# A fused attention and MLP-mixer kernel on one core: two stores move to Gelu's buffers, a PSUM copy is cut in halves, reciprocals are spread a turn later, and row maxima are placed a little later behind VectorE

## The chip, the core and the metric

The kernel runs on one core of a Trainium2 chip. The core has TensorE (PE in the profile, with its weight loads as PEld), VectorE (DVE), ScalarE (ACT), GpSimd (POOL), and SyncE (SP), which here only issues transfers. Each engine works through its own queue in order, and semaphores tie the queues together. Matmuls write to PSUM, which has eight banks of 128 partitions x 512 float32 values.

The metric is the device time of one execution in microseconds. Before the change the median of three runs is 1082.11 us (1080.81, 1086.48 and 1082.11).

## The reference

The input x has 2048 tokens of width 448. A gate per token mixes an attention block of 16 heads (28 wide) with an MLP that has a layer norm in front and 1792 hidden units. All is float32.

```python
def _A_ref(x, wqkv, wo):
    qkv = (x @ wqkv).reshape(B, S, 3, H, Dh).transpose(2, 0, 3, 1, 4)
    q, k, v = qkv[0], qkv[1], qkv[2]
    scores = jnp.einsum("bhqd,bhkd->bhqk", q, k) * (Dh ** -0.5)
    p = _softmax(scores, axis=-1)
    o = jnp.einsum("bhqk,bhkd->bhqd", p, v)
    return o.transpose(0, 2, 1, 3).reshape(B, S, D) @ wo

def _B_ref(x, w1, b1, w2, b2):
    y = _layernorm(x, axis=-1)
    h = _gelu(jnp.einsum("bsd,df->bsf", y, w1) + b1)
    return jnp.einsum("bsf,fd->bsd", h, w2) + b2

g = _sigmoid((x * gate_w).sum(-1, keepdims=True))
return g * _A_ref(x, A_wqkv, A_wo) + (1 - g) * _B_ref(x, B_w1, B_b1, B_w2, B_b2)
```

## The kernel before

To stay near float32 the kernel splits an operand into a high part (fp32r, a reduced form) and a low part, the rest, and adds three products: high by high, high by low, low by high.

The work has two stretches. The **first** makes queries, keys and values and then the whole MLP. TensorE's 128 rows are used as four strips of 32 rows; each strip works on its own share of an output tile, and four matmuls, one a strip, run side by side. The MLP goes block by block, four blocks of 512 tokens: 14 "up" tiles (hidden units, class `Up`), each emptied by ScalarE with Gelu into a tile `h` and copied to its high part, and then four "down" tiles (class `Down`, 128 tokens each), emptied by ScalarE into a tile `gb` (L398) and stored to memory (`gbs`, L401) until the end. `h` has two buffers, and `gb` has two. Only in the last block do the third and fourth down tile (`self.i > 1`) use the buffers of `h`. When a tile is asked for, the next buffer in turn is given, and its first writer waits until the last reader, a store here, is done with it.

The order of TensorE's matmuls in this stretch is made while the program is built, by a planner (`Strips`). It keeps a clock for each strip and a time at which each engine is free, with a fixed cost for each kind of work, and gives a strip the first work that is ready by these clocks. Work left over for it are the **row maxima** (`RowMax`): the softmax needs for each query the largest score over 2048 keys, so a matmul of queries against 512 keys is made into PSUM bank 6 or 7 (L212) and VectorE reduces it to one column (L214). There are 1024 of these in all. `rowmax` (L497 to L508) places one when a strip comes by and one of the two banks is free by the planner's reckoning, which is when VectorE is done (`self.dve`, 0.65 for a reduction) and a margin later. What is not placed here is made in the second stretch.

The **second** stretch is attention. A unit is one head's scores of 128 keys against 512 queries: three matmuls and an exp on ScalarE. There are 1024 units, 64 for each of 16 combinations of four heads and 512 queries (`n`). Work goes by **turns** (`turn_of`): a turn has five, six or seven units in two halves, and among their passes stand row maxima that are still owed (`lone`): three in a turn of five (at places 0, 3 and 5; the first and third use bank 6), two in a turn of six (places 0 and 5, both bank 6). As long as more than a certain number are owed, the size is five. After the scores of a turn come that turn's entries of an agenda (transfers and small work that was put down for it), and then **batches**: the products of four units' probabilities with values, 128 keys for four heads (`batch`), summed in bank 7 over 16 batches. When the last of the 16 is done, `valued` runs: `finish_a` copies bank 7 to `ob` on VectorE (L1026), and SyncE gathers the row sums out of it (`lt`). Two turns after that `finish_b` takes reciprocals on VectorE, stores them to memory (`rls`) and loads them four times, spread over 32 partitions each (`rc`, L1037). Four turns after, `finish_c` multiplies `ob` by `rc` on GpSimd. In the last group of heads the result is split and projected with the output weights on TensorE (`project`, L1004 to L1006).

Of the kernel before, what the change touches and what calls it, by code (L numbers as in the profile page):

```python
# [15 lines left out]
P = 128  # L16
# [3 lines left out]
DH = 28  # L20
F = 1792
NG = 4
CH = 512
NC = S // CH
# [11 lines left out]
def kernel(ctx: ExitStack, tc: tile.TileContext, xt, wqk, wv, wo, xk, w1, b1, w2, b2,  # L36
                          ident_d, sel_d, out):
    nc = tc.nc
# [21 lines left out]
    rls = dram.tile([NG * NC, 4, CH], F32, name="rls")  # L60
# [101 lines left out]
    class RowMax:  # L162
# [64 lines left out]
        def close(self, n):  # L227
            mf, mt = self.mf[n % 2], self.mt[n % 2]
            nc.vector.reduce_max(mf[:, 0:16], self.mx[n % 2].rearrange("p j i k -> p (j i) k"), axis=AX)
            nc.vector.transpose(mt, mf)  # L230
# [138 lines left out]
    class Down(Piece):  # L369
# [21 lines left out]
            return st.hready.get((self.c, f, p), 1e9) > now or self.c == 0 and st.w2ready.get(f, 1e9) > now  # L391

        def close(self, st, now):
            if self.c == NC - 1 and self.i > 1:
                gb = mhp[0].tile([P, CH], F32, name="h", bufs=2)[:, :D]
            else:
                gb = mhp[0].tile([P, D], F32, name="gb", bufs=2)
            nc.scalar.activation(gb, bk[:, self.bank, :D], AF.Copy)  # L398
            st.use("act", now + 0.2, 0.56)
            st.free[self.bank] = st.act + 0.1  # L400
            nc.scalar.dma_start(gbs[self.c * TPC + self.i], gb)  # L401
            st.use("act", now, 0.5)

    class Strips:
# [28 lines left out]
        def at(self, t, fn, **uses):  # L433
            self.tasks.append((t, self.count, fn, uses))
            self.count += 1
# [61 lines left out]
        def rowmax(self, s, now):  # L497
            if now < self.hot[s] or not rowmax.ready(s):
                return False
            if rowmax.cnt[s] > 5 + min(rowmax.cnt):  # L500
                return False
            b = min(self.rm, key=lambda b: self.rm[b])
            if self.rm[b] > now:
                return False
            ends = rowmax.one(s, bk[:, b])
            self.t[s] = now + 0.232
            self.use("dve", now + 0.45, RM)
            self.rm[b] = self.dve + 0.1  # L508
            for kind, n, j in ends:
                if kind == "q":  # L510
                    self.at(now + 6.0, lambda n=n, j=j: rowmax.load_q(n, j))
                elif kind == "k":
                    def load(n=n, j=j):
                        rowmax.load_k(n, j)
                        self.hot[j] = self.get(self.clock + 0.6, 224) + 1.0

                    self.at(now + 1.5, load)
                    self.hot[j] = 1e9
                else:
                    self.at(now + 0.5, lambda n=n: rowmax.close(n), dve=0.45)  # L520
                    self.at(now + 3.0, lambda n=n: rowmax.store(n))
            return True
# [370 lines left out]
    for i, key in enumerate(load):  # L893
        r = slots[i % 8]
# [48 lines left out]
    def turn_bank(i):  # L943
        return (i + shift) % 6
# [47 lines left out]
    def split_o(g, c, o):  # L992
        if c not in ohs:
            ohs[c] = ao.tile([P, NG, CH], F32R, name="oh"), ao.tile([P, NG, CH], F32R, name="ol")
        h, l = (t[:, g] for t in ohs[c])
        nc.gpsimd.tensor_copy(h, o)
        nc.gpsimd.tensor_sub(l, o, h.bitcast(F32))
# [20 lines left out]

    pv = bk[:, 7]
    obs = {}  # L1020

    def finish_a(n):
        ob = ao.tile([P, CH], F32, name="ob", bufs=1)
        lt = ao.tile([P, CH // 32], F32, name="lt")
        obs[n] = ob, lt
        nc.vector.tensor_copy(ob, pv)  # L1026
        nc.sync.dma_start(lt, ob[DH:P:32, :])

    def finish_b(n):
        ob, lt = obs[n]  # L1030
        rc = ao.tile([P, CH], F32, name="rc", bufs=1)
        obs[n] = ob, rc
        nc.vector.reciprocal(lt, lt)
        r = rls[n]
        nc.sync.dma_start(r.rearrange("j (a b) -> (j a) b", b=CH // 32), lt)
        for j in range(4):
            nc.sync.dma_start(rc[32 * j:32 * j + 32], r[j].partition_broadcast(32))  # L1037

    def finish_c(n):
        g, c = divmod(n, NC)  # L1040
        ob, rc = obs.pop(n)
        if g < NG - 1:
            nc.gpsimd.tensor_mul(ot[g][:, c * CH:(c + 1) * CH], ob, rc)
            return
        nc.gpsimd.tensor_mul(ob, ob, rc)
        split_o(g, c, ob)
# [53 lines left out]
    def valued(n, turn):  # L1100

        g, c = divmod(n, NC)
        if n == NG * NC - 1:
            finish_last(n)
            return
        finish_a(n)
        at(turn + 2, lambda: finish_b(n))
        at(turn + 4, lambda: finish_c(n))
        if g == NG - 1:
            for i in range(TPC):  # L1110
                tail.append((turn + 6 + i, c * TPC + i))
# [7 lines left out]
    def lone(s, b, turn):  # L1119
        if not rowmax.ready(s) or turn < cold[s]:  # L1120
            return
        for kind, n, j in rowmax.one(s, bk[:, b]):
            if kind == "q":
                at(turn + 1, lambda n=n, j=j: rowmax.load_q(n, j))
            elif kind == "k":
                at(turn + 1, lambda n=n, j=j: rowmax.load_k(n, j))
                cold[j] = turn + 5
            else:
                at(turn + 1, lambda n=n: rowmax.close(n))
                at(turn + 2, lambda n=n: rowmax.store(n))  # L1130

    def turn_of(u, turn):

        left = UNITS - u
        owed = rowmax.left()
        size = 5 if owed and owed > 2 * ((left - 104) // 6) + 6 * sixes[0] else 6
        sixes[0] = size == 6
        if not owed and not (tail and tail[0][0] <= turn + 1):
            size = 7
        size = min(left, size)  # L1140
        na = min(4 if size == 7 else 3, size)
        nb = size - na
        for x in range(u, u + size):
            n = x // 64
            if n not in begins:
                begins.add(n)
                begun(n, turn)
        extra = {5: ((0, 3, 6), (3, 1, 5), (5, 2, 6)), 6: ((0, 3, 6), (5, 2, 6))}.get(size, ())
        if size == 7:
            sevens.append(turn)  # L1150
        place = (lambda i: i) if sevens else turn_bank
        if turn in projected:
            extra = extra[1:]
        for half, first, count in ((0, 0, na), (1, na, nb)):
            for p in range(3):
                for x, o, b in extra:
                    if x == 3 * half + p:
                        lone((u + o) % 4, b if b == 6 else turn_bank(b), turn)
                for i in range(first, first + count):
                    n, k = divmod(u + i, 64)  # L1160
                    k, j = divmod(k, 4)
                    r = slice(32 * j, 32 * j + DH + (p == 0))
                    ks = slice(k * P, (k + 1) * P)
                    w = (khi, klo, khi)[p][n // NC]
                    q = (qh, qh, ql)[p][n % 3]
                    nc.tensor.matmul(bk[:, place(i)], w[r, ks], q[r], start=(p == 0), stop=(p == 2), skip_group_check=True)  # L1166
            if count:
                t = ap.tile([P, 4 - half, CH], F32, name=f"p{half}")
                b = place(first)
                nc.scalar.activation(t[:, :count], bk[:, b:b + count], AF.Exp, scale=SCALE)  # L1170
                for i in range(count):
                    prob[u + first + i] = t[:, i]
        return size

    def batch(b, turn, sl=slice(0, CH)):
        n, k = divmod(b, NT)
        for j in range(4):
            nc.tensor.matmul(bk[32 * j:32 * j + 32, 7, sl], vg[n // NC][:, k, 32 * j:32 * j + 32], prob[4 * b + j][:, sl],  # L1178
                             start=(k == 0), stop=(k == NT - 1), skip_group_check=True)
        if k == NT - 1 and sl.stop == CH:  # L1180
            valued(n, turn)
            return True
        return False
# [3 lines left out]
    while b < UNITS // 4:  # L1187
# [12 lines left out]
        while 4 * b + 4 <= before and quota:  # L1200
# [7 lines left out]
            b, begun_half = b + 1, False  # L1208
# [59 lines left out]
```

## Time and profile before

| what | value |
|---|---|
| median of 3 runs | 1082.11 us |
| profiled execution | 1083.55 us |
| its span (first to last instruction) | 1081.8 us |
| TensorE busy | 1068.8 us, 13450 matmuls |
| VectorE busy | 740.8 us, of that 673.7 in 1024 reductions (L214) |
| ScalarE busy | 634.0 us, of that 481.1 in exp (L1170) |
| GpSimd busy | 368.3 us |
| first score of attention | 452.2 us after the start |
| granted clock of TensorE | 1.00, 0.98 after 1010 us |

A row of the timeline or of the groups names the line of the kernel, the engine, the operation, and the tile written and read (`bk` is PSUM, all eight banks under one name); a timeline row begins with its start and its duration in us, and ends with the idle time before it and what ended it. A merged row ends in xN. In a row of waits stand the waiting and the releasing work, then us in total, times, and the longest. In a row of windows each engine's busy time in the stretch is followed by its count. The ends of matmuls are modelled, and matmuls of different strips overlap.

### The profile page before, as it was taken

The page shows a single profiled execution, that of the slowest core. Times are in us where ns is not written, and L with a number is a line of the kernel's source. Part 1 is how long each engine was busy: PE and PEld are TensorE (multiplying, and loading weights), DVE is VectorE, ACT ScalarE, POOL GpSimd, SP SyncE. Part 2 cuts the span into 40 slices and gives each one's busy share as a digit, 9 for nine tenths or more (in the row PEclk, how much of TensorE's full clock was granted, in tenths as well). Part 3 has the DMA queues.
Part 4 walks back from the last instruction along what each step waited for, and adds up shares of the span by engine and source line. Part 5 has one row for each costly group of instructions (what it writes and reads, how often), then busy time and mean ns, then how long its engine had stood idle before and what let it go on. Part 6 is the DMA issues. An engine that isn't in the chain of part 4 may idle for free.

```text
span 1081.8 us, 31072 instructions
## 1 busy us (share of the span) xinstructions
PE 1068.8 (99%) x13450; PEld 725.4 (67%) x13450; DVE 740.8 (68%) x1186; ACT 634.0 (59%) x654; POOL 368.3 (34%) x388
## 2 busy tenths in 40 slices
PE   9999999999999999999999999999999999999997
PEld 6999999999999899844444444444444444464555
DVE  4899998999999999876667655676664444422102
ACT  5234463042142033288788788778888888857671
POOL 4565577336244037441001101300110332444431
PEclk9999999999999999999999999999999999999999
DMA  6696433212100104220000011310000301011111
GB/s 232 214 269 217 168 111 104 77 46 61 45 7 7 46 12 118 92 77 18 25 11 27 16 31 38 78 41 6 25 26 23 71 27 50 25 55 36 61 47 67
DMA packets 47785, 73.20 MB, mean 68 GB/s; under 512 B 13840, under 2 KB 28816, under 8 KB 46848
## 3 DMA queue, kind: packets, MB, share of 16 engines
q1 hardware_dynamic: 33888, 39.11, 12.4%
q0 software_dynamic: 5120, 16.89, 5.5%
q10 hardware_dynamic: 8640, 15.21, 3.9%
q8 instruction: 105, 1.72, 0.7%
q14 instruction: 32, 0.26, 0.1%
HBM read 51.75 MB, written 19.31 MB: 66 GB/s over the span
## 4 chain that ended last, share of the span: by engine, by line
PE 95%; ACT 2%; DMA 2%; DVE 1%; issue 1%; SPq 0%; DVEq 0%; ACTq 0%
PE bk L488 34%; PE bk L1178 22%; PE bk L1166 18%; PE bk L212 15%; PE bk L1004 1%; ACT p L1170 1%; PE bk L1005 1%; PE bk L1006 1%; DMA gbs<-gb 1%; PE bk L920 1%; DMA first<-in_xt 1%; ACT gb L398 0%; DVE ob L1026 0%; PE bk L948 0%; DVE mx L214 0%
## 5 line engine op out<-in xcount | busy, mean ns | idle before, releaser
L214 DVE TENSOR_REDUCE mx<-bk 128x1 f32<-128x512 f32 x1024 | 673.7, 688 | 221.8 <-PE bk L212 178.6
L1170 ACT ACTIVATE p<-bk 128x1536 f32<-128x1536 f32 (+1 forms) x381 | 481.1, 1315 | 125.8 <-PE bk L1166 125.1
L212 PE MATMUL bk<-kd,qd 28*128 28x512 f32 x1024 | 449.8, 441 | 0.6 <-DVE mx L214 0.2
L212 PEld LDWEIGHTS bk<-kd,qd 28*128 28x128 f32 x1024 | 186.0, 182 | 179.7 <-DVE mx L214 115.1
L488 PE MATMUL bk<-yh,w1f 32*128 32x512 f32 x1568 | 192.9, 393 | 2.2 <-ACT gb L398 2.2
L488 PE MATMUL bk<-yl,w1f 32*128 32x512 f32 x784 | 167.4, 392 | 0.0
L488 PEld LDWEIGHTS bk<-yh,w1f 32*128 32x128 f32 x1568 | 154.6, 183 | 4.9 <-ACT gb L398 3.4
L488 PE MATMUL bk<-w2h,hh 32*128 32x448 f32 x896 | 145.0, 366 | 0.0
L488 PE MATMUL bk<-w2l,hh 32*128 32x448 f32 x896 | 144.1, 363 | 0.0
L1178 PE MATMUL bk<-p,va 128*32 128x512 f32 (+1 forms) x1144 | 130.2, 556 | 0.0
L1178 PE MATMUL bk<-p,vb 128*32 128x512 f32 (+1 forms) x1184 | 129.2, 542 | 0.0
L363 POOL TENSOR_TENSOR hl<-h,hh 128x512 fp32r<-128x512 f32 x56 | 72.4, 1305 | 137.2 <-ACT hh L356 99.7
L840 POOL CAST yh<-yl 128x512 fp32r<-128x512 f32 x16 | 9.8, 611 | 288.0 <-DMA yl<-qk 131.2
L488 PEld LDWEIGHTS bk<-yl,w1f 32*128 32x128 f32 x784 | 105.8, 183 | 0.3
L488 PEld LDWEIGHTS bk<-w2l,hh 32*128 32x128 f32 x896 | 103.1, 183 | 0.3
L488 PEld LDWEIGHTS bk<-w2h,hh 32*128 32x128 f32 x896 | 102.7, 183 | 0.4
L1166 PE MATMUL bk<-yh,ka 29*128 29x512 f32 x512 | 101.1, 483 | 0.5 <-ACT p L1170 0.5
L1166 PE MATMUL bk<-yh,kb 29*128 29x512 f32 x512 | 96.5, 480 | 1.7 <-ACT p L1170 1.7
L488 PE MATMUL bk<-w2h,hl 32*128 32x448 f32 x896 | 93.1, 362 | 0.0
L398 ACT ACTIVATE gb<-bk 128x448 f32<-128x448 f32 x14 | 7.6, 545 | 136.8 <-PE bk L488 129.7
L1166 PE MATMUL bk<-yh,la 28*128 28x512 f32 x512 | 83.4, 393 | 0.0
L488 PEld LDWEIGHTS bk<-w2h,hl 32*128 32x128 f32 x896 | 82.4, 183 | 0.3
(141 smaller groups left out, 1604.5 us busy)
## 6 DMA issues: line engine op xcount, KB each, us to landing
qk<-qo ACTq DMA_DIRECT2D x28, 256.0 KB
raw<-in_xt SPq DMA_DIRECT2D x17, 256.0 KB
vs<-vt ACTq DMA_DIRECT2D x16, 256.0 KB
rc<-rls SPq DMA_DIRECT2D x60, 64.0 KB
bxr<-in_xk POOLq DMA_DIRECT2D x8, 448.0 KB, 6.4
acc<-gbs SPq DMA_DIRECT2D x16, 224.0 KB
out_y<-acc SPq DMA_DIRECT2D x16, 224.0 KB
qd<-qk SPq DMA_DIRECT2D x60, 56.0 KB
```

The lines of the kernel that those rows point to most:

```text
L212: nc.tensor.matmul(ps, self.qd[n % 2][r, i * P:(i + 1) * P], self.kd[r, k * 512:(k + 1) * 512], start=True, stop=True)
L214: nc.vector.reduce_max(self.mx[n % 2][:, j, i, k:k + 1], ps, axis=AX)
L363: nc.gpsimd.tensor_sub(hl[f], h, hh[f].bitcast(F32))
L488: mm = nc.tensor.matmul(bk[:, x.bank, :n], a, b, start=x.first, stop=(len(x.rem) == 1 and m == len(ops) - 1), skip_group_check=True)
L840: nc.gpsimd.tensor_copy(h, l.bitcast(F32))
L920: nc.tensor.matmul(bk[:, b], w, v, start=(i == 0), stop=(i == len(ops) - 1), skip_group_check=True)
L1004: nc.tensor.matmul(po, h, woh[:, g], start=(g == 0), stop=False, skip_group_check=True)
L1005: nc.tensor.matmul(po, h, wol[:, g], start=False, stop=False, skip_group_check=True)
L1006: nc.tensor.matmul(po, l, woh[:, g], start=False, stop=(g == NG - 1), skip_group_check=True)
L1166: nc.tensor.matmul(bk[:, place(i)], w[r, ks], q[r], start=(p == 0), stop=(p == 2), skip_group_check=True)
L1170: nc.scalar.activation(t[:, :count], bk[:, b:b + count], AF.Exp, scale=SCALE)
L1178: nc.tensor.matmul(bk[32 * j:32 * j + 32, 7, sl], vg[n // NC][:, k, 32 * j:32 * j + 32], prob[4 * b + j][:, sl], start=(k == 0), stop=(k = ...
```

## The change

There are four parts.

1. The third and fourth down tile of every block, not only of the last one, are emptied into the buffers of `h`.
2. The planner's margin after which a row maximum's bank counts as free is 0.15 instead of 0.1. This is a number in the planner's reckoning and no instruction; it moves the places of row maxima in the first stretch, and what is placed around them.
3. The copy of bank 7 is made in two halves of 256 columns. The second half, and the gather of the row sums behind it, comes in the next turn, after that turn's first row maximum (or at the turn's end, if none stands there).
4. The four loads that spread the reciprocals come a turn later than the store of the reciprocals, through a function of their own.

```diff
@@ class Down, close @@
-            if self.c == NC - 1 and self.i > 1:
+            if self.i > 1:
                 gb = mhp[0].tile([P, CH], F32, name="h", bufs=2)[:, :D]
             else:
                 gb = mhp[0].tile([P, D], F32, name="gb", bufs=2)
@@ Strips.rowmax @@
-            self.rm[b] = self.dve + 0.1
+            self.rm[b] = self.dve + 0.15
@@
+    late = []

     def finish_a(n):
         ob = ao.tile([P, CH], F32, name="ob", bufs=1)
         lt = ao.tile([P, CH // 32], F32, name="lt")
         obs[n] = ob, lt
-        nc.vector.tensor_copy(ob, pv)
-        nc.sync.dma_start(lt, ob[DH:P:32, :])
+        nc.vector.tensor_copy(ob[:, :CH // 2], pv[:, :CH // 2])
+
+        def rest():
+            nc.vector.tensor_copy(ob[:, CH // 2:], pv[:, CH // 2:])
+            nc.sync.dma_start(lt, ob[DH:P:32, :])
+
+        late.append(rest)
+
+    def copy_rest():
+        while late:
+            late.pop()()

     def finish_b(n):
...
-        r = rls[n]
-        nc.sync.dma_start(r.rearrange("j (a b) -> (j a) b", b=CH // 32), lt)
+        nc.sync.dma_start(rls[n].rearrange("j (a b) -> (j a) b", b=CH // 32), lt)
+
+    def spread_rc(n):
         for j in range(4):
-            nc.sync.dma_start(rc[32 * j:32 * j + 32], r[j].partition_broadcast(32))
+            nc.sync.dma_start(obs[n][1][32 * j:32 * j + 32], rls[n][j].partition_broadcast(32))
@@ valued @@
         finish_a(n)
         at(turn + 2, lambda: finish_b(n))
+        at(turn + 3, lambda: spread_rc(n))
         at(turn + 4, lambda: finish_c(n))
@@ turn_of @@
                     if x == 3 * half + p:
                         lone((u + o) % 4, b if b == 6 else turn_bank(b), turn)
+                        copy_rest()
...
+        copy_rest()
         return size
```

Three places in the order of instructions. The first is ScalarE's queue at the end of the MLP's block 1: four down tiles are emptied and stored, and the first Gelu of block 2 follows. Before:

```order
L398 ACTIVATE gb_6384<-bk_115 128x448
L401 DMA gbs_90<-gb_6384 128x448
L398 ACTIVATE gb_6390<-bk_115 128x448
L401 DMA gbs_90<-gb_6390 128x448
L398 ACTIVATE gb_6420<-bk_115 128x448
L401 DMA gbs_90<-gb_6420 128x448
L398 ACTIVATE gb_6429<-bk_115 128x448
L401 DMA gbs_90<-gb_6429 128x448
L355 ACTIVATE h_6481<-bk_115,b1s_64 128x512
```

And after the change:

```order
L398 ACTIVATE gb_6349<-bk_115 128x448
L401 DMA gbs_90<-gb_6349 128x448
L398 ACTIVATE gb_6365<-bk_115 128x448
L401 DMA gbs_90<-gb_6365 128x448
L398 ACTIVATE h_6408<-bk_115 128x448
L401 DMA gbs_90<-h_6408 128x448
L398 ACTIVATE h_6426<-bk_115 128x448
L401 DMA gbs_90<-h_6426 128x448
L355 ACTIVATE h_6478<-bk_115,b1s_64 128x512
```

The third and fourth emptying now take the two buffers of `h`, which the next Gelu takes in turn after them; the third no longer follows the first in a buffer of `gb`.

The second place is VectorE's queue around the first copy of bank 7 in attention. Before:

```order
L214 TENSOR_REDUCE mx_155<-bk 128x1 x33
L1026 COPY ob<-bk 128x512
L214 TENSOR_REDUCE mx_155<-bk 128x1 x6
L1033 RECIPROCAL lt<-lt 128x16
L214 TENSOR_REDUCE mx_155<-bk 128x1 x4
```

And after the change:

```order
L214 TENSOR_REDUCE mx_155<-bk 128x1 x18
L1027 COPY ob<-bk 128x256
L214 TENSOR_REDUCE mx_155<-bk 128x1
L1030 COPY ob<-bk 128x256
L214 TENSOR_REDUCE mx_155<-bk 128x1 x5
L1043 RECIPROCAL lt<-lt 128x16
L214 TENSOR_REDUCE mx_155<-bk 128x1 x24
```

One reduction has moved between the two halves; the reciprocal still has six reductions between it and the copy's first half.

The third place is TensorE's queue in attention's turn 120 (L212 is a row maximum, L1166, after the change L1179, a pass of scores, with their count). Before:

```order
L212 MATMUL bk<-kd,qd_152 128x512
L1166 MATMUL bk<-yh,ka 128x512 x3
L1166 MATMUL bk<-yh,la 128x512 x3
L1166 MATMUL bk<-yl,ka 128x512 x3
L1166 MATMUL bk<-yh,ka 128x512 x3
L1166 MATMUL bk<-yh,la 128x512 x3
L212 MATMUL bk<-kd,qd_152 128x512
L1166 MATMUL bk<-yl,ka 128x512 x3
```

And after the change:

```order
L212 MATMUL bk<-kd,qd_152 128x512
L1179 MATMUL bk<-yh,ka 128x512 x3
L1179 MATMUL bk<-yh,la 128x512 x3
L1179 MATMUL bk<-yl,ka 128x512 x3
L212 MATMUL bk<-kd,qd_152 128x512
L1179 MATMUL bk<-yh,ka 128x512 x2
L1179 MATMUL bk<-yh,la 128x512 x2
L212 MATMUL bk<-kd,qd_152 128x512
L1179 MATMUL bk<-yl,ka 128x512 x2
```

The turn of six units with two row maxima has become a turn of five with three: 566 row maxima stand ahead of the first score, where 578 did, so the change to turns of six comes twelve turns later.

## The prediction

> **What bounds the kernel now.** I read the page first: its engine row, and its chain of work that ended last.
>
> ```profile
> span 1081.8 us, 31072 instructions
> ...
> PE 1068.8 (99%) x13450; PEld 725.4 (67%) x13450; DVE 740.8 (68%) x1186; ACT 634.0 (59%) x654; POOL 368.3 (34%) x388
> ...
> PE 95%; ACT 2%; DMA 2%; DVE 1%; issue 1%; SPq 0%; DVEq 0%; ACTq 0%
> ```
>
> TensorE carries 95% of the chain. Its queue is in order, so time is lost in two ways only: when TensorE gets more to do, and when the instruction at its head waits. The number of its instructions does not change. What changes is where 12 row maxima stand, and what a few heads wait for. So next I ask where the maxima stand now (windows of line 212, the maxima's matmuls, cut at the first score), and how tight VectorE is while they are made (windows of all engines, MLP block 1).
>
> ```profile
> 0.00:452.20 452.20, 242.23 (x578) 105.02 (x578) 1.00 0.34 105
> 452.20:1082.00 629.80, 207.60 (x446) 80.98 (x446) 1.00 0.14 41
> ```
> ```profile
> core 0: us, PE busy (x) PEld busy (x) DVE busy (x) ACT busy (x) POOL busy (x), PEclk, DMA share, GB/s
> 213.00:294.00 81.00, 80.35 (x1388) 76.77 (x1385) 78.93 (x124) 22.15 (x37) 33.87 (x27) 1.00 0.17 51
> ```
>
> 578 maxima are ahead of attention, 446 inside it. In block 1, TensorE issues 1388 matmuls in 81.00 us, one per 58 ns (four strips side by side), and VectorE is busy for 78.93 of 81.00 us. The granted clock is 1.00.
>
> **Attention's turns.** The timeline shows a plain turn of five units (472.50 to 475.21), the batches of values in a turn with one and in a turn with two, a turn with the copy of the values (493.22 to 496.20), and a turn of six (808.56 to 811.70).
>
> ```profile
> 472.50 0.50 PE L212 MATMUL bk<-kd,qd 28*128 28x512 f32 x1
> 473.04 1.99 DVE L214 TENSOR_REDUCE mx<-bk 128x1 f32<-128x512 f32 x3 [0.71 <-PE bk L212]
> 473.78 0.50 PE L212 MATMUL bk<-kd,qd 28*128 28x512 f32 x1
> 474.22 1.06 PE L1178 MATMUL bk<-p,va 128*32 128x512 f32 x8
> 475.21 0.49 PE L212 MATMUL bk<-kd,qd 28*128 28x512 f32 x1
> 476.92 1.92 PE L1178 MATMUL bk<-p,va 128*32 128x512 f32 x16
> ...
> 493.22 0.50 PE L212 MATMUL bk<-kd,qd 28*128 28x512 f32 x1
> 493.42 0.69 DVE L1026 COPY ob<-bk 128x512 f32<-128x512 f32 x1 [0.37 <-PE bk L1178]
> 494.03 1.96 DVE L214 TENSOR_REDUCE mx<-bk 128x1 f32<-128x512 f32 x3
> 494.77 0.50 PE L212 MATMUL bk<-kd,qd 28*128 28x512 f32 x1
> 496.20 0.50 PE L212 MATMUL bk<-kd,qd 28*128 28x512 f32 x1
> ...
> 808.56 0.49 PE L212 MATMUL bk<-kd,qd 28*128 28x512 f32 x1
> 810.27 1.50 PE L1178 MATMUL bk<-p,va 128*32 128x256 f32 x16
> 811.70 0.50 PE L212 MATMUL bk<-kd,qd 28*128 28x512 f32 x1
> ```
>
> A plain turn of five takes 475.21 - 472.50 = 2.71 us. A second batch adds 1.92 - 1.06 = 0.86. Without its batch the turn of five takes 1.85. The turn of six takes 811.70 - 808.56 = 3.14 and holds one and a half batches (1.29), so it also takes 1.85 without them. A turn therefore costs the same for five units with three maxima as for six units with two. That is what makes a maximum dear in attention.
>
> **Part 1: maxima placed 0.15 behind VectorE instead of 0.1.** This number moves places only. Counted in the written order, 566 maxima stand ahead of the first score, not 578. Attention then has 136 turns of five and 49 of six, where it had 124 and 59. That is two more turns, with batches unchanged: 2 x 1.85 = **+3.7 us**. Against it, the stretch ahead loses 12 matmuls of 58 ns: **-0.7 us**. If VectorE sets that stretch's pace, each maximum taken out would give what a reduction takes in a row of three, 1.99 / 3 = 0.66 us: 12 x 0.66 = 8 us. That is one bound, and nothing the other. I take -0.7, because the waits between 138 and 452 us show TensorE almost never held by a reduction:
>
> ```profile
> PEld bk L212 <- DVE mx L214: 0.6, 2, 0.3
> ```
>
> **Part 2: Gelu's buffers for the stores of two down tiles.** At the end of each of the first three blocks, ScalarE empties four down tiles through two buffers, and one of them must wait until an earlier tile has landed in memory. The timeline of ScalarE at the ends of blocks 1 and 2, and the waits:
>
> ```profile
> 290.22 0.33 ACTq L401 DMA_DIRECT2D gbs<-gb  x1
> ...
> 292.90 0.54 ACT L398 ACTIVATE gb<-bk 128x448 f32<-128x448 f32 x1 [1.71 <-DMA gbs<-gb]
> ...
> 295.51 0.69 ACT L355 ACTIVATE h<-bk,b1s 128x512 f32<-128x512 f32 x1 [1.06 <-PE bk L488]
> ```
> ```profile
> 371.88 0.33 ACTq L401 DMA_DIRECT2D gbs<-gb  x1
> ...
> 376.03 0.54 ACT L398 ACTIVATE gb<-bk 128x448 f32<-128x448 f32 x1 [3.18 <-DMA gbs<-gb]
> ```
> ```profile
> ACT gb L398 <- DMA gbs<-gb: 6.7, 4, 3.2
> ...
> PEld bk L488 <- ACT gb L398: 3.4, 3, 1.8
> ...
> PE bk L488 <- ACT gb L398: 2.2, 3, 1.4
> ```
>
> ScalarE waits 6.7 us in four places. The bank that it holds keeps the next block's first matmuls, and all behind them in TensorE's queue, back three times: 2.2 us by the matmul rows, 3.4 by the weight loads. I take 3.2, nearer the loads, since the matmuls' ends are modelled. With four buffers instead of two no down tile waits: **-3.2 us**.
>
> What is late next: the next block's first Gelu outputs use the same two buffers, so now they wait for the stores. A store lands 2.7 us (290.22 to 292.90) to 4.2 us (371.88 to 376.03) after its issue. In block 1 the first Gelu began 2.6 us after the third emptying (292.90 to 295.51), and the issue follows that by 0.6. Gelu would be late by 0.7 to 2.2 us there; at the end of block 2 a little, of block 0 not. Behind it on ScalarE stand only the next Gelu and its copy; TensorE waits only if it wants that very bank first, and the down tiles have just freed four others. Bounds 0 and 2.2; I take **+0.4**.
>
> [...]
>
> **Part 3: the copy in halves.** In the plain turn the third maximum starts 473.78 - 472.50 = 1.28 us in, just behind the first reduction, whose bank it reuses. In the turn with a copy the reductions start 0.61 later than the copy, and the third maximum starts 494.77 - 493.22 = 1.55 in. So one copy costs 0.27 us. The half's own cost is not in the trace; the nearest rows:
>
> ```profile
> L1026 DVE COPY ob<-bk 128x512 f32<-128x512 f32 x15 | 10.4, 691 | 13.5 <-PE bk L1178 13.5
> ...
> L1071 DVE TENSOR_TENSOR ob<-ob,bk 128x128 f32<-128x128 f32 x4 | 1.1, 281 | 2.1 <-PE bk L1068 2.1
> ```
>
> Between 281 ns for 128 columns and 691 for 512, 256 columns come to 281 + 128 x 410/384 = 418 ns. Of the whole copy 0.61 of 0.69 shows ahead of the next reduction; of the half then some 0.34. The bounds are 0.28 and 0.42.
>
> The first reduction now begins 0.20 + 0.34 = 0.54 in, as in a plain turn, and the 0.27 is gone. But VectorE has the second half yet to do: 0.20 + 0.34 + 0.64 (reduction) + 0.34 + 0.64 + 0.69 = 2.85. The next turn's first maximum takes the bank of the last reduction, so it cannot start before about 2.90. In a turn with one batch this replaces 2.98 by 2.90, a gain of 0.08 only. With two batches, or with six units, the turn is longer than that and keeps the whole 0.27. In the new order six copies fall in turns of five with one batch and eight in longer ones (the fifteenth, in a turn of seven, delays nothing): 6 x 0.08 + 8 x 0.27 = 2.6; I take **-2.5 us**. The bounds are -3.8 (all fourteen whole) and, with halves of 0.42 (end at 3.01, next turn at 3.06), 6 x 0.08 - 2.2 = -1.7.
>
> [...]
>
> **Part 4: denominators spread a turn later.** SyncE's queue holds the four spreading transfers behind the store of the reciprocals. They move past the transfers of that turn's agenda: row-maximum queries, keys, maxima rows. The lengthening of the copy delays the gather ahead of them by 0.7 us. TensorE needs the products only in the last group; the tightest is the second last tile:
>
> ```profile
> 988.62 1.28 POOL L1045 TENSOR_TENSOR ob<-ob,rc 128x512 f32<-128x512 f32 x1 [3.31 <-DMA rc<-rls]
> ...
> 990.66 1.27 POOL L997 TENSOR_TENSOR ol<-ob,oh 128x512 fp32r<-128x512 f32 x1
> ...
> 996.96 0.47 PE L1004 MATMUL bk<-woh,oh 128*128 128x448 f32 x1
> ```
>
> GpSimd is ready at 991.93, TensorE begins at 996.96: 5.0 us of cover against one turn (about 3.1 in turns of six). **Nothing**; with the cover gone, up to 3 us.
>
> **The sum**: +3.7 - 0.7 - 3.2 + 0.4 - 2.5 = **-2.3 us**. The profiled execution took 1083.55 us, 1.4 above the median of the runs, 1082.11; it would become 1081.2. Against the median I predict **1079.8 us**, 0.2% less. About 0.5%, 5.4 us, is what a measurement can tell from no change.
>
> **The rivals.**
> VectorE paces the stretch ahead of attention: then part 1 gives -8 there, and the sum is -9.6, 1072.5 us. For it: VectorE busy 78.93 of 81.00 us in block 1. Against it: 0.6 us of waits. Chance 0.10.
> Slower: the wait on the stores only moves from the down tiles to Gelu, which stands at the head of ScalarE's queue just when the new block wants banks. If TensorE is held for the full 2.2 us at each of three block ends, 6.6 in place of 0.4, the sum is +3.9: 1086.0. It decides once those stalls pass 2.7 us together. For it: stores of 4.2 us, and the three stalls of today are of this kind. Against it: block 0 leaves more than 3 us. Chance 0.12.
> The halves do nothing, since in each copy's turn VectorE ends later than TensorE: sum +0.2, 1082.3. For it: 2 x 0.42 + 1.99 = 2.83 us of VectorE work in a turn of 2.71. Against it: eight of fourteen turns are longer. Chance 0.18.
> The forecast: 0.52, with its own range 1077 to 1083. What I have not named: 0.08.
>
> **How the numbers follow.** The range, 1075 to 1085, holds forecast and third rival, and parts of the other two. Faster by over 0.5% (under 1076.7) takes the first rival and the forecast's lower edge: 0.17. Slower by over 0.5% (over 1087.5) takes the unnamed and the second rival's tail: 0.07. Within: 0.76.
>
> **What would show it.** Part 1: 566 maxima before the first score, two more turns after it. Part 2: no wait of the emptying on a store, and Gelu waiting on one at the end of block 1. Part 3: third maximum at 1.28 in turns with a copy, turns of 2.90 or 3.56. Part 4: projections starting without a wait on GpSimd. I am wrong if the first score comes over 8 us earlier (VectorE was the pace), or if TensorE's waits on Gelu's emptying pass 2.7 us.

## The result, and the profile after

The changed kernel has a median of 1085.53 us (1082.89 to 1087.26, 22 runs), where the kernel before, run beside it, has 1082.46 us (22 runs). The ratio is 1.0019, with a 95% interval of 1.0010 to 1.0028: about 2.1 us slower (the medians lie 3.1 us apart). Of the 22 executions, 15 show a mean granted clock of 0.995 to 0.998 (median 1085.72 us) and seven one of 0.999 or 1.000 (median 1083.46 us); the profiled one is of the first kind. The forecast was 1079.8 us, 2.3 us faster, with a range that ended at 1085. It was right that the change is within 0.5%, and wrong about the sign. The sum was off by about 4.4 us, and the experiments were to find where.

The page of the changed kernel, profiled in an execution of 1084.87 us:

```profile
span 1083.1 us, 31036 instructions
...
PE 1070.2 (99%) x13410; PEld 733.3 (68%) x13410; DVE 742.5 (69%) x1201; ACT 634.5 (59%) x658; POOL 368.6 (34%) x388
...
PE 95%; ACT 2%; DMA 2%; issue 1%; DVE 1%; ACTq 0%; DVEq 0%
```

The page as a whole says little: the same 95% on TensorE as before. TensorE has 40 matmuls fewer (13410 against 13450), where the prediction said that their number does not change: a turn of six makes one and a half batches, so every two of them split a batch into two halves of 256 columns, eight matmuls more for the same columns, and ten turns of six are gone. The windows of line 212, split at the first score, say more.

```profile
0.00:450.18 450.18, 235.11 (x566) 103.32 (x566) 1.00 0.35 106
450.18:1083.00 632.82, 211.78 (x458) 83.00 (x458) 1.00 0.14 40
```

566 maxima stand ahead of the first score, as counted from the order. The first score comes 2.05 us earlier than before (450.18 against 452.23), and what follows takes 3.4 us longer (632.9 against 629.5). The first 0.94 us of the earlier start is a difference of start-up between the two executions: the first maximum begins at 28.00 us here, and at 28.94 in before.

**A stall that was not there.** The waits of the first 140 us name a line of which the prediction says nothing, L295, where ScalarE empties a bank with queries or keys into a tile `qo` (four buffers), whose store to memory follows at L299.

```profile
ACT qo L295 <- DMA qk<-qo: 7.2, 2, 3.8
...
PEld bk L488 <- ACT qo L295: 2.8, 1, 2.8
PE bk L488 <- ACT qo L295: 2.4, 1, 2.4
```

ScalarE's timeline around it, first in the changed kernel (start, duration, instruction, and in brackets the idle time ahead of it and what ended that):

```profile
71.27 0.60 ACT L295 ACTIVATE qo<-bk 128x512 f32<-128x512 f32 x1 [3.39 <-DMA qk<-qo]
71.90 0.33 ACTq L299 DMA_DIRECT2D qk<-qo  x1
73.44 1.09 ACT L295 ACTIVATE qo<-bk 128x512 f32<-128x512 f32 x2 [1.58 <-PE bk L488]
...
75.95 0.60 ACT L295 ACTIVATE qo<-bk 128x512 f32<-128x512 f32 x1 [1.42 <-PE bk L488]
...
80.83 0.60 ACT L295 ACTIVATE qo<-bk 128x512 f32<-128x512 f32 x1 [3.76 <-DMA qk<-qo]
```

and in the kernel before:

```profile
70.41 1.28 ACT L295 ACTIVATE qo<-bk 128x512 f32<-128x512 f32 x2 [1.14 <-DMA sel<-in_sel]
71.15 0.89 ACTq L299 DMA_DIRECT2D qk<-qo  x2
76.53 0.60 ACT L295 ACTIVATE qo<-bk 128x512 f32<-128x512 f32 x1 [4.84 <-PE bk L488]
...
78.60 0.60 ACT L295 ACTIVATE qo<-bk 128x512 f32<-128x512 f32 x1 [0.44 <-PE bk L488]
...
79.81 0.58 ACT L295 ACTIVATE qo<-bk 128x512 f32<-128x512 f32 x1
```

A fifth tile takes the buffer of the first. In before it comes 8.7 us after the issue of that buffer's store (71.15 to 79.81), and waits for nothing. In the changed order four tiles are emptied between 71.27 and 76.55, and ScalarE is ready for the fifth at 80.83 - 3.76 = 77.07. The store issued at 71.90 lets go only at 80.83, 8.9 us later. The bank that the fifth tile holds is wanted by TensorE, whose queue stands meanwhile:

```profile
78.72 0.38 PE L488 MATMUL bk<-xh,wq 32*128 32x512 f32 x1
81.48 0.47 PE L488 MATMUL bk<-wvs,xh 32*128 32x450 f32 x1 [2.37 <-ACT qo L295]
```

The same stretch in windows of 2 us (length; busy time and instructions of PE, PEld, DVE, ACT, POOL; granted clock; DMA share; GB/s):

```profile
78.00:80.00 2.00, 1.11 (x20) 0.68 (x13) 1.29 (x2) 0.00 (x0) 0.62 (x2) 1.00 1.07 380
80.00:82.00 2.00, 0.52 (x9) 0.52 (x13) 0.00 (x0) 1.17 (x3) 0.00 (x0) 1.00 1.03 377
82.00:84.00 2.00, 2.00 (x29) 2.00 (x28) 1.41 (x3) 1.50 (x3) 1.93 (x3) 0.58 0.86 302
84.00:86.00 2.00, 2.00 (x28) 2.00 (x25) 1.30 (x2) 0.00 (x0) 1.82 (x4) 0.56 0.57 150
86.00:88.00 2.00, 2.00 (x42) 1.91 (x37) 1.87 (x4) 1.42 (x3) 1.98 (x4) 1.00 0.05 14
```

The DMA engines are full (share 1.07 and 1.03) while the store takes so long. The stall is 81.48 - 78.72 = 2.76 us from start to start, and behind it TensorE works at a granted clock of 0.58 and 0.56 for 4 us, with 29 and 28 matmuls in 2 us where the next 2 us have 42. By these windows that takes another 4 x 0.43 = 1.7 us, an estimate. Together that would be 4.5 us.

**The passage to attention.** The third place is the first score itself. TensorE's timeline, changed kernel:

```profile
450.18 0.50 PE L1179 MATMUL bk<-yh,ka 29*128 29x512 f32 x2
450.93 0.49 PE L1179 MATMUL bk<-yh,ka 29*128 29x512 f32 x1 [0.25 <-ACT h L398]
...
451.94 0.49 PE L1179 MATMUL bk<-yh,ka 29*128 29x512 f32 x1
...
454.42 0.49 PE L212 MATMUL bk<-kd,qd 28*128 28x512 f32 x1
```

and in the kernel before:

```profile
452.23 0.84 PE L1166 MATMUL bk<-yh,ka 29*128 29x512 f32 x4
...
455.42 0.49 PE L212 MATMUL bk<-kd,qd 28*128 28x512 f32 x1
```

Turn 0 takes 454.42 - 450.18 = 4.25 us (from unrounded starts). Before it took 3.19, from 452.23 to 455.42. TensorE now comes to the scores earlier than ScalarE is done with the last down tiles, whose emptyings begin at 450.33 and 451.34 and hold two of the banks. That is 1.06 us, given back where the first stretch had gained it.

### The profile page after: what moved, and what is told of

Read it like the earlier page. It is cut to its first block, busy times and chain, and to the rows that moved or that the text cites. A ratio compares the mean times of both kernels' runs of the same rounds, so it can differ in the third digit from the quotient of the medians.

```text
span 1083.1 us, 31036 instructions
## 1 busy us (share of the span) xinstructions
PE 1070.2 (99%) x13410; PEld 733.3 (68%) x13410; DVE 742.5 (69%) x1201; ACT 634.5 (59%) x658; POOL 368.6 (34%) x388
## 4 chain that ended last, share of the span: by engine, by line
PE 95%; ACT 2%; DMA 2%; issue 1%; DVE 1%; ACTq 0%; DVEq 0%
PE bk L488 34%; PE bk L1192 22%; PE bk L1179 19%; PE bk L212 15%; ACT p L1183 1%; PE bk L1004 1%; DMA qk<-qo 1%; PE bk L1005 1%; PE bk L1006 1%; PE bk L920 1%; PE bk L905 0%; DMA out_y<-acc 0%; DVE acc L1011 0%; DVE mx L214 0%; ACT qo L295 0%
## 5 line engine op out<-in xcount | busy, mean ns | idle before, releaser
L1183 ACT ACTIVATE p<-bk 128x1536 f32<-128x1536 f32 (+2 forms) x385 | 481.5, 1304 | 127.3 <-PE bk L1179 120.6
L212 PE MATMUL bk<-kd,qd 28*128 28x512 f32 x1024 | 446.9, 438 | 0.4 <-DVE mx L214 0.2
L212 PEld LDWEIGHTS bk<-kd,qd 28*128 28x128 f32 x1024 | 186.3, 182 | 175.0 <-DVE mx L214 119.8
L488 PE MATMUL bk<-yh,w1f 32*128 32x512 f32 x1568 | 190.1, 392 | 0.2 <-ACT h L355 0.2
L488 PEld LDWEIGHTS bk<-w2h,hh 32*128 32x128 f32 x896 | 106.4, 183 | 0.1
L1179 PE MATMUL bk<-yh,ka 29*128 29x512 f32 x512 | 103.3, 482 | 0.7 <-ACT p L1183 0.4
L1179 PE MATMUL bk<-yh,kb 29*128 29x512 f32 x512 | 96.5, 480 | 1.5 <-ACT p L1183 1.3
L1179 PE MATMUL bk<-yh,la 28*128 28x512 f32 x512 | 85.4, 393 | 0.0
L488 PEld LDWEIGHTS bk<-w2h,hl 32*128 32x128 f32 x896 | 84.8, 183 | 0.2
L1179 PE MATMUL bk<-yl,ka 28*128 28x512 f32 x512 | 84.1, 408 | 0.0
```

The costliest lines, as they stand in the source:

```text
L212: nc.tensor.matmul(ps, self.qd[n % 2][r, i * P:(i + 1) * P], self.kd[r, k * 512:(k + 1) * 512], start=True, stop=True)
L488: mm = nc.tensor.matmul(bk[:, x.bank, :n], a, b, start=x.first, stop=(len(x.rem) == 1 and m == len(ops) - 1), skip_group_check=True)
```

## The experiments

All ratios are against the kernel before, run on the same chip beside each experiment, with 95% intervals.

### What the new margin alone does, and what all else does without it

The first run is the changed kernel with the margin back at 0.1, the second the kernel before with the margin at 0.15 and nothing else.

```diff
-            self.rm[b] = self.dve + 0.15
+            self.rm[b] = self.dve + 0.1
```

> The changed kernel with the planner's margin back at 0.1; buffers, halves and the later spreading stay. Theory A (the loss is part 1's: a new stall of 4.3 us near 80 us, two more turns, a dearer junction): all that goes, and parts 2 and 3 are left with what the profile of the changed kernel showed of them, -3.4 for the stores and -2.5 for the halves: about 5.7 us under the kernel before, near 1076.7, no stall near 80 us. Theory B (the halves or Gelu's buffers cost something that the two profiles do not show side by side): within 2 us of the kernel before.

> The kernel before with the margin 0.15 alone. Theory A: the changed kernel's time plus what parts 2 and 3 gave: some 8 us over the kernel before, near 1090, with the same stall near 80 us (2.7 us at one matmul) and 566 maxima ahead. Theory B: as the changed kernel, 3 us over the kernel before. If the stall near 80 us is chance of one execution it is not in this profile, and the time is near 1086.

Without the margin the changed kernel is faster than the kernel before: 0.9951 (0.9938 to 0.9964), median 1078.84 us. The margin alone makes the kernel before slower: 1.0083 (1.0068 to 1.0098), 1092.67 us. Against the whole change the first is 0.0068 less, 7.4 us: so much does part 1 cost in the changed kernel, where the prediction had +3.0 (+3.7 - 0.7). Parts 2, 3 and 4 together bring 0.49%, 5.3 us, where the prediction had -5.3 (-3.2 + 0.4 - 2.5). So it is part 1 that was mis-sized. In the kernel before the margin costs 9.0 us (0.0083), 1.6 more than in the changed kernel: there a down tile's wait on a store, which Gelu's buffers take away, holds TensorE for another 2.2 us near 215 us, and a second stretch of slow clock follows (216.51 to 219.92 us, shown in the last section). The kernel with the margin alone shows the same wait as the changed kernel, at the same place:

```profile
ACT qo L295 <- DMA qk<-qo: 4.0, 1, 4.0
...
PE bk L488 <- ACT qo L295: 2.7, 1, 2.7
```
```profile
80.00:85.00 5.00, 2.47 (x32) 2.46 (x35) 1.51 (x3) 2.67 (x5) 1.87 (x3) 0.84 0.99 331
85.00:90.00 5.00, 5.00 (x78) 4.86 (x74) 4.14 (x7) 2.15 (x4) 4.72 (x8) 0.82 0.51 124
```

### A fifth buffer: the stall taken away, the order kept

To test whether the wait on the store is the cause, the changed kernel gets a fifth buffer for `qo`; another small tile gives its fifth buffer up for want of room.

```diff
-    po = p0.enter_context(tc.tile_pool(name="po", bufs=4))
+    po = p0.enter_context(tc.tile_pool(name="po", bufs=5))
@@
-    vt = [px.tile([P, H, 32], F32, name=f"vt{i}") for i in range(5)]
+    vt = [px.tile([P, H, 32], F32, name=f"vt{i}") for i in range(4)]
@@
-            v, ps, tt = vt[self.i % 5], bk[:, self.bank], self.i
+            v, ps, tt = vt[self.i % 4], bk[:, self.bank], self.i
```

> The changed kernel with five instead of four buffers for the queries and keys on their way to memory (and four instead of five for the values, for want of room); the order of matmuls is the same. If the stall near 80 us comes from ScalarE waiting for the store of four tiles ago, it goes: no wait of the emptying on a store there, TensorE's clock 1.00 throughout, and some 4 us under the changed kernel, near 1081.3. If the stall is DMA traffic that holds TensorE in another way, or not the cause, the time stays near 1085.5.

Measured: 0.9969 (0.9957 to 0.9980), 1080.36 us. That is 0.0050 below the changed kernel, 5.4 us, with the same written order. In the windows the stall and the slow clock are gone:

```profile
75.00:80.00 5.00, 5.00 (x93) 4.89 (x91) 4.67 (x10) 3.02 (x6) 2.42 (x4) 1.00 1.02 382
80.00:85.00 5.00, 5.00 (x94) 4.93 (x91) 4.97 (x9) 3.33 (x7) 4.82 (x8) 1.00 1.04 350
85.00:90.00 5.00, 5.00 (x86) 4.71 (x81) 4.93 (x10) 0.86 (x3) 4.67 (x8) 1.00 0.56 199
```

Counted from the same instruction in both (the emptying at 61.94 us in the changed kernel, 63.09 here), the first score comes 388.24 and 383.93 us later: the stall costs 4.3 us, close to the 4.5 read off above. (Single traces carry some noise here: four kernels of these experiments with one and the same order in the first stretch took 419.8 to 421.4 us from the first maximum to the first score.) With DMA just as full, share 1.02 and 1.04, nothing is held up. So the full DMA engines alone do not hold TensorE up; it takes too few buffers for the time that a store then needs (8.9 us in the changed kernel).

The rest, 1.0 us, is in attention (632.9 against 631.9), where the fifth buffer has no work. Five pairs of turns, 29/30, 61/62, 93/94, 125/126 and 157/158, each take 0.27 us longer in the changed kernel and in the kernel with the margin alone than here; one other turn takes 0.36 us longer here. The view of the exponentials' line (L1183) shows another releaser in four of these places; its lists of what ScalarE waited for, first the changed kernel, then this one:

```profile
  PE bk L1179: 120.6, 182
  PE bk L212: 5.9, 4
```
```profile
  PE bk L1179: 125.0, 186
```

The view infers that four exponentials waited for a maximum's matmul. The order of the instructions in ScalarE's queue, semaphore waits included, shows something else. In all five places ScalarE's wait for the scores is over (at 537.60 us in the first), and the exponential still starts only 0.32 to 0.34 us later, where here it starts after 0.04 us. From one of these places to the next the queue holds exactly 128 instructions, and 0.65 to 0.9 us behind each late start a transfer of 8 KB of instructions begins (at 538.60, 632.34, 726.50, 820.58 and 920.78 us). So the five late starts stand 128 instructions apart, in the pairs of turns that take 0.27 us longer; what delays them is not shown. With the fifth buffer the queue holds one semaphore wait less ahead of attention, the same exponentials stand one place earlier, and none of them comes late. For the buffer that is luck; no run shifts the queue by an instruction and does nothing else.

### Twelve maxima fewer ahead, at the old margin

If the two further turns are the price of leaving 12 maxima to attention, then the kernel before, made to stop at 566, must pay it without the margin.

```diff
-            if rowmax.cnt[s] > 5 + min(rowmax.cnt):
+            if sum(rowmax.cnt) >= 566 or rowmax.cnt[s] > 5 + min(rowmax.cnt):
```

> The kernel before, whose planner stops at 566 maxima ahead of attention: the last 12 are left to attention, and nothing else moves before them. It measures the price of 12 maxima by itself. By the turns: two more turns 3.7, less 0.7 ahead: 3.0 us over the kernel before, 1085.5. If VectorE paces the end of the first stretch (12 x 0.66 saved), 4 us under it.

Measured: 1.0025 (1.0015 to 1.0035), 1086.11 us, +2.7 us, where the prediction's two terms give +3.0. Attention is 3.5 us longer (633.1 against 629.5; predicted +3.7), and the first score comes at 450.31, 1.9 us earlier. The rival by which VectorE paces the first stretch wanted 8 us there. It falls.

The sum comes out, but not by two more turns. Counted in the traces, the kernel before has 191 turns, the changed kernel 193, and this one 192: its last turn holds four units instead of one and takes 2.1 us longer to the end, and its turn 0 takes 0.6 us longer (3.77 against 3.19). The changed kernel with the fifth buffer and the one with margin 0.1 differ in attention by the two turns and turn 0 alone: 631.9 - 626.8 = 5.1 us, of which turn 0 is 1.1. That leaves 4.0 us for the two turns, where the prediction had 3.7.

### Gelu's buffers alone, the whole copy, and the early spread

Three kernels take parts 2, 3 and 4 apart: the kernel before with part 2 alone; the changed kernel at the old margin with the copy made whole again; and the changed kernel at the old margin with the spread where it was.

```diff
-            if self.c == NC - 1 and self.i > 1:
+            if self.i > 1:
```

> The kernel before with Gelu's buffers for the third and fourth down tile of every block, and nothing else. The three stalls of 0.7, 1.0 and 1.7 us at the ends of the blocks go and no wait on a store comes in their place: 3.3 us under the kernel before, ratio 0.997. Rival: the wait moves to Gelu: ratio 0.999 to 1.000 and rows of Gelu waiting on a store. If this ratio equals that of the kernel with the whole copy, the later spreading gives nothing.

```diff
-        nc.vector.tensor_copy(ob[:, :CH // 2], pv[:, :CH // 2])
-
-        def rest():
-            nc.vector.tensor_copy(ob[:, CH // 2:], pv[:, CH // 2:])
-            nc.sync.dma_start(lt, ob[DH:P:32, :])
-
-        late.append(rest)
+        nc.vector.tensor_copy(ob, pv)
+        nc.sync.dma_start(lt, ob[DH:P:32, :])
```

> Margin 0.1, Gelu's buffers and the later spreading, but the copy of bank 7 whole again. Against the kernel with margin 0.1 and halves (0.9951 of the kernel before) it tells what the halves give: 0.27 us in each of nine longer turns and 0.17 in five turns of five with one batch by that profile, 3.0 us; so some 2.4 us under the kernel before, ratio 0.998. If the halves give nothing, 0.995.

```diff
-        at(turn + 3, lambda: spread_rc(n))
+        at(turn + 2, lambda: spread_rc(n))
```

> Margin 0.1, Gelu's buffers and the halves, but the four spreading transfers right behind the store of the reciprocals, as in the kernel before. If part 4 costs and gives nothing, ratio 0.995, as with margin 0.1 and all the rest. If it gives something, nearer to 1.

Part 2 alone: 0.9973 (0.9963 to 0.9983), -2.9 us; the prediction had -3.2 + 0.4 = -2.8. Its trace shows no wait on a store of a down tile any more. The changed kernel shows one, and it is the wait that the prediction named, of the first Gelu at the end of block 1 (waits from 138 to 458 us):

```profile
ACT h L355 <- DMA gbs<-h: 1.6, 1, 1.6
...
PEld bk L488 <- ACT h L355: 0.8, 2, 0.7
...
PE bk L488 <- ACT h L355: 0.2, 1, 0.2
```

1.6 us of ScalarE lie within the 0.7 to 2.2 of the prediction, and TensorE pays 0.2 to 0.8 for it. The rival that this wait holds TensorE for 2.2 us at each of three block ends falls.

Part 3: with the whole copy 0.9974 (0.9963 to 0.9984), with halves 0.9951, a difference of 0.0023, 2.5 us, and attention takes 629.4 and 626.8 us. The prediction had -2.5. The intervals of the two ratios touch at 0.9963 and 0.9964, so the size rests on the turns too. A turn with a copy in the changed kernel:

```profile
492.24 0.49 PE L212 MATMUL bk<-kd,qd 28*128 28x512 f32 x1
...
492.45 0.42 DVE L1027 COPY ob<-bk 128x256 f32<-128x256 f32 x1 [0.39 <-PE bk L1192]
...
492.79 0.68 DVE L214 TENSOR_REDUCE mx<-bk 128x1 f32<-128x512 f32 x1
...
493.38 0.41 DVE L1030 COPY ob<-bk 128x256 f32<-128x256 f32 x1
...
493.52 0.50 PE L212 MATMUL bk<-kd,qd 28*128 28x512 f32 x1
...
493.72 1.28 DVE L214 TENSOR_REDUCE mx<-bk 128x1 f32<-128x512 f32 x2
...
495.05 0.18 PEld L212 LDWEIGHTS bk<-kd,qd 28*128 28x128 f32 x1 [0.92 <-DVE mx L214]
```

The third maximum stands 1.28 us into the turn, as predicted, and each half shows 0.34 us ahead of the next reduction (492.45 to 492.79, 493.38 to 493.72), as predicted. VectorE ends 495.00 - 492.24 = 2.76 us in, and the turn takes 2.81 us, against a predicted 2.90 and 2.98 before. So VectorE does bind here, as the third rival had it, but the turn still gains 0.17 us instead of 0.08. The four turns with two batches gain 0.27 (3.84 to 3.57), as predicted, and so does one of the turns of six (3.41 to 3.14); a later one gains 0.17 (3.83 to 3.66), and the two others nothing (3.52 and 4.11, as before). That makes 6 x 0.17 + 5 x 0.27 + 0.17 = 2.5 us. The changed kernel's groups of the two halves:

```profile
L1027 DVE COPY ob<-bk 128x256 f32<-128x256 f32 x15 | 6.4, 425 | 13.6 <-PE bk L1192 13.6
L1030 DVE COPY ob<-bk 128x256 f32<-128x256 f32 x15 | 6.2, 415 | 0.0
```

The estimate between two rows of before was 418 ns. The turn gains since only 0.34 us of a half's 0.42 keeps the next reduction back.

Part 4: the early spread gives 0.9953 (0.9939 to 0.9967) where the late one gives 0.9951, and the kernel with part 2 and the late spread (0.9974) stands beside that with part 2 alone (0.9973). It moves nothing, as predicted.

### Other margins

What the margin does seems to hang on which waits the order meets, and not on the count of maxima alone. Three kernels try it: the changed kernel at 0.12, the same with the fifth buffer, and the changed kernel at 0.09.

```diff
-            self.rm[b] = self.dve + 0.15
+            self.rm[b] = self.dve + 0.12
```

> The changed kernel with margin 0.12: 569 maxima ahead of attention and one more turn than in the kernel before. If a maximum's place costs only turns: 1.9 us over the kernel with margin 0.1, ratio 0.997. If a stall on a store of queries and keys or another new wait comes with every other order of the first stretch, 4 us more, ratio 1.000 or above.

> Margin 0.12 with five buffers for queries and keys (four for the values), the rest as changed; same order as with margin 0.12 alone. That kernel's profile shows no emptying of queries or keys waiting on a store and no stall near 80 us, so a fifth buffer should give nothing: ratio 0.993 as before. If it is lower by 0.002 or more, waits too short for the view held TensorE there.

```diff
-            self.rm[b] = self.dve + 0.15
+            self.rm[b] = self.dve + 0.09
```

> The changed kernel with margin 0.09. It leaves 468 maxima to attention by the written order, as many as margin 0.15 does, so the two more turns are there (3.7 us over margin 0.1). If maxima ahead decide the time: ratio 0.998. If what decides is which waits the order meets in the first stretch, and this order meets none near 80 us, it can be lower than 0.995 in spite of the turns.

| margin | maxima ahead | first score, us | attention, us | median, us | ratio (95%) |
|---|---|---|---|---|---|
| 0.09 | 565 | 444.96 | 631.9 | 1078.66 | 0.9968 (0.9955 to 0.9980) |
| 0.10 | 578 | 450.34 | 626.8 | 1078.84 | 0.9951 (0.9938 to 0.9964) |
| 0.12 | 569 | 445.18 | 629.3 | 1076.49 | 0.9933 (0.9921 to 0.9945) |
| 0.12, fifth buffer | 569 | 445.44 | 629.2 | 1076.44 | 0.9942 (0.9929 to 0.9955) |
| 0.15 | 566 | 450.18 | 632.9 | 1085.53 | 1.0019 (1.0010 to 1.0028) |
| 0.15, fifth buffer | 566 | 447.02 | 631.9 | 1080.36 | 0.9969 (0.9957 to 0.9980) |

(Margin 0.09 leaves 1024 - 565 = 459 maxima to attention and 0.15 leaves 458; the 468 of the expectation is a slip.) Neither the count ahead nor the time goes up or down steadily with the margin. At 0.12 there is no wait for the store of a `qo` tile, and there a fifth buffer gives nothing; at 0.15 it gives 5.4 us, 4.3 of them the stall. So the fifth buffer is worth what the stall costs, beside the chance shift in ScalarE's queue. The changed kernel at 0.12 beats both kernels: 0.67% faster than the kernel before, about 9 us below the change as made. Its interval overlaps that of 0.10.

One thing stays open here. At 0.12 the first score comes 5.2 us earlier than at 0.10 (from the first maximum 416.8 us, against 419.8 to 421.4 in the four traces of the order at 0.10), with nine maxima fewer, and hardly any wait of TensorE tells the two apart. The windows from 138 to 213 us, first at 0.10, then at 0.12:

```profile
138.00:213.00 75.00, 74.47 (x1255) 71.62 (x1250) 68.87 (x107) 28.58 (x49) 50.03 (x41) 1.00 0.34 93
```
```profile
138.00:213.00 75.00, 75.00 (x1306) 73.21 (x1301) 68.33 (x108) 28.92 (x51) 50.47 (x41) 1.00 0.36 101
```

TensorE is busy nearly throughout in both, and the second issues 4% more matmuls (1306 against 1255) in the same time. The two stretches don't hold quite the same instructions, and two other traces of the order at 0.10 show 1265 and 1271, so this is no proof; it points to how closely the matmuls follow each other, and not to waits. Which property of the order does it was not tried.

## Why the prediction was right or wrong, point by point

The step that failed is the opening of part 1: "This number moves places only", taken as a reason that moved places cost nothing, and with it the sum's entry for the first stretch, "the stretch ahead loses 12 matmuls of 58 ns: -0.7 us". I priced the count of maxima and looked at no place to which things were moved. In the sum part 1 had +3.0 us; it cost 7.4. What stood in the place of that entry was a wait: with the moved order a fifth `qo` tile comes before the first one's store has landed, and the stall, with the slow clock behind it, costs 4.3 us, which a fifth buffer takes away.

| term | predicted, us | measured, us |
|---|---|---|
| two more turns in attention | +3.7 | +4.0 (fifth buffer against margin 0.1, without turn 0) |
| 12 maxima out of the first stretch, and what else moved there | -0.7 | about -2.5, a remainder |
| stall on the store of a `qo` tile, with the slow clock behind it | not in the sum | +4.3 |
| turn 0, banks still held by the last down tiles | not in the sum | +1.1 |
| exponentials that start late in ScalarE's queue | not in the sum | +1.0 |
| Gelu's buffers, with the late Gelu | -2.8 | -2.9 |
| copy in halves | -2.5 | -2.5 |
| denominators spread later | 0 | 0 |
| sum | -2.3 | +2.5; the ratio says +2.1 |

The remainder is worked out thus: from the first maximum to the first score the changed kernel takes 1.1 us less than before (450.18 - 28.00 against 452.23 - 28.94); the stall adds 4.3 and Gelu's buffers take off 2.9, so 2.5 are left. The kernel stopped at 566 shows 1.7 of it (421.6 against 423.3 us from the first maximum), and traces of one order differ by up to 1.6, so there may be nothing more to find. It is not traced to rows.

- Part 1, turns: right in count, and nearly in price.
- Part 1, the first stretch and its end: wrong by three things that were absent from the sum. A part of one, the slow clock behind the stall (0.50 from 82.33 to 85.74 us), lies outside the "two ways only" in which the prediction saw time lost. How long the store takes could not be read off the kernel before: there the same store was done within the 8.7 us that the fifth `qo` tile came behind it, and nothing shows by how much. But the DMA share of 1.04 around it was on view. The prediction quotes the waits from 138 us on only, where the maxima are dense, and took what lies before for untouched.
- Part 2: right, both in gain and in what came late next.
- Part 3: the sum right, its split not: the turns with one batch gained twice what I gave them, two of the longer ones nothing.
- Part 4: right.
- The rivals: VectorE's pace fell by the kernel stopped at 566; the stall of TensorE behind Gelu fell by 0.2 to 0.8 us; that the halves do nothing fell by 2.5 us. The slower outcome came by the kind of mechanism that the second rival has, a wait on a store that holds a bank, but at a place that I had not named and in another tile, and from another part of the change. I had given such a thing 0.08.

## What to carry to other kernels

A number that only sets places in an order written out by a planner is not costed by counting what changes sides: go through the places to which other instructions were moved, and for each rotating buffer compare the time from a store's issue to the buffer's next use with what a store takes in that very stretch. Where before shows no wait, it may have missed one by little. And when such a number is tuned, tell the wait that it meets from the number's own effect: a buffer more, with the order of TensorE kept, nearly does it in one run.

## What the runs showed of the hardware

A store of one 128x512 tile of 32-bit numbers, 256 KB, held its buffer for 8.9 us (71.90 to 80.83) while the DMA share stood at 1.02. The stores of down tiles, 224 KB, let go after 2.7 and 4.2 us at shares of 0.47 and 0.33. The prediction had used only the latter.

The granted clock steps at 82.33, 85.74 and 1082.43 us in the changed kernel, and at 83.39, 86.80, 216.51 and 219.92 in the one with the margin alone. The distances are whole multiples of 3.413 us: 85.74 - 82.33 = 3.41, 1082.43 - 85.74 = 292 x 3.413, and 216.51 - 83.39 = 39 x 3.413. So the windows below begin and end a whole multiple of 3.413 us from such a step. First the stall in the changed kernel, then two places in the kernel with the margin alone:

```profile
78.92:82.33 3.41, 1.04 (x20) 0.85 (x20) 0.66 (x2) 1.50 (x3) 0.26 (x1) 1.00 1.04 370
82.33:85.74 3.41, 3.41 (x42) 3.41 (x38) 2.17 (x4) 1.17 (x3) 3.23 (x6) 0.50 0.68 207
```
```profile
213.09:216.51 3.42, 1.71 (x28) 1.28 (x20) 2.20 (x4) 0.29 (x2) 0.00 (x0) 1.00 0.38 139
216.51:219.92 3.41, 2.95 (x28) 2.42 (x32) 1.11 (x2) 0.95 (x2) 0.00 (x0) 0.50 0.36 135
...
298.42:301.84 3.42, 2.12 (x35) 1.63 (x32) 2.02 (x4) 0.77 (x2) 0.00 (x0) 1.00 0.20 71
```

After a window in which PE was busy for 1.04 or 1.71 us of 3.41, the next one runs at half the clock (0.50). After the one with 2.12 it does not (the next shows 1.00). In the kernel before, a stall near 375 us has 0.52 and 0.83 us of idle time in two such windows next to each other (372.39 to 375.80 and 375.80 to 379.21), and the clock stays at 1.00. So in these traces 1.71 us of idle time in a window went with half the clock in the next, and 1.30 us did not; none of the windows shown lies between, and no run varies the idle time alone. The stall of 2.76 us cost 4.3 here. Whether it leaves the clock alone when it is split over two windows was not tried; the seven executions with a mean clock of 0.999 or 1.000 would fit that, but no trace of one was kept. The 0.98 after 1010 us in the kernel before is a stretch at 0.50 as well: it begins at 1078.94 us, and the last matmul ends at 1076.62.
